# Two accumulators in turn for the inner sums, and a borrowed one for the scores

## The chip, the cores and the metric

One core of a Trainium2 chip runs the whole program. Its engines are named as the profile names them: PE multiplies matrices (PEld is its loading of weights), DVE, ACT and POOL work on vectors, and SP issues most transfers. The metric is device time in microseconds. Three runs of the kernel before took 1115.9, 1118.8 and 1119.08 us, with a median of 1118.8 us.

## The reference

The reference is block-causal attention, and then a feed-forward layer with a gate on all its outputs:

```
scores = q @ k^T / 8                      # 8 batches x 8 heads, 576 x 64 each, float32
scores = where(block_i >= block_j, scores, -1e9)      # blocks of 64 positions
attn   = exp(scores - rowmax); attn = attn / (rowsum + 1e-9)
x      = (attn @ v), heads side by side   # 4608 tokens x 512
h      = x @ w_in                         # 512 x 2048
g      = h * sigmoid(1.702 h)
out    = g @ w_out                        # 2048 x 512
```

## The kernel before

**Attention** goes by pairs of heads; a pair is called a turn here, as in the code, and there are 32, numbered from 0. The scores of a turn stand in five row chunks of growing width (64, 192, 320, 448 and 576 columns). `score` makes them in groups: PE writes the scores of both heads to PSUM banks, `weigh` reduces them on DVE (mask, scale, row minimum; in the profile L351) and takes the exponential on ACT (L358), and `normalise` multiplies by the reciprocal of the row sum, on POOL or DVE. From the ninth turn on `turn` transposes the result on DVE (L385, L390) into `turned`, and after the widest chunk SP issues 16 transfers (L397) that put it into the order in which `av` reads it. `av` multiplies by the values one turn later, and ACT copies the outcome to `xr`.

**The feed-forward layer** goes by 12 tiles of 384 tokens, and by 16 pieces of the 2048 inner columns in each. For each piece PE makes an *inner sum* `hp` (12 matmuls of 384 columns, one PSUM bank), which ACT (tanh, L562) and DVE (L563) turn into `g`; ACT rounds it to `gh` (L571), POOL makes the rest `gl` (L82), and PE adds three products for each of three 128-token blocks to the *outer sums* `acc0` to `acc2` (9 matmuls of 512 columns). Operands are split into a high and a low part, hence three products for each.

**Order.** PE's order is fixed by the code: `keep_in_program_order` holds every matmul where it was written. Inner and outer sums come from a generator that is advanced between the steps of a turn (`advance`). From the tenth turn on a turn is `"3+0/2+1 - - - V - - 4 - - - L -"`: one score group of chunks 3 and 0 and of 2 and 1, then the values of the turn before (`V`), then the widest chunk 4 as a group, then the next turn's q and k (`L`). The generator stops only where an inner sum has just been made, so a score group stands between an inner sum and the outer sum of the piece before. Six inner sums fall into each turn. They are called *first* to *sixth* here, counted from the score group 3+0/2+1: first, second, `V`, third, fourth, score group 4, fifth, sixth. The order on DVE, ACT and POOL is made by a scheduler from priorities and dependencies; `tc.high_priority` favours the gate (tanh, `g`, `gh`, `gl`).

**PSUM** has eight banks. Three hold `acc0` to `acc2`, one (`h`) holds every inner sum in turn, and four (`w0` to `w3`) go round for scores and values from the tenth turn on. `w3` serves the conversion of the weights before that. A tile that takes a bank waits until all that read the bank's last tile are done.

Of the kernel before, what the change touches and what calls it, by code (L numbers as in the profile page):

```python
# [10 lines left out]
F32 = mybir.dt.float32  # L11
# [29 lines left out]
def attention_moe_kernel(  # L41
# [12 lines left out]
    P = 128  # L54
# [9 lines left out]
    HP = H // 2  # L64
# [4 lines left out]
    ps = ctx.enter_context(tc.tile_pool(name="ps", bufs=1, space=PSUM))  # L69
# [4 lines left out]
    def early(n):  # L74

        return n < 2 * HP
# [7 lines left out]


    turns = {"n": 0, "bank": 0, "experts": False}
    conv = {"step": 0, "loaded": 0}

    def bank():
        tags = ["w0", "w1", "w2"]  # L90
        if not turns["experts"]:
            tags += ["acc0", "acc1", "acc2", "h"]
        elif turns["n"] > 2 * HP:
            tags.append("w3")
        turns["bank"] += 1
        return ps.tile([P, 512], F32, tag=tags[turns["bank"] % len(tags)], name="bank")

    def mm(**kw):
        return tc.keep_in_program_order(nc.tensor.matmul(**kw))  # L99
# [65 lines left out]
    def width(i):  # L165
        return BLK * (2 * i + 1)

    def qrange(i):
        return (0, BLK) if i == 0 else (BLK * (2 * i - 1), BLK * (2 * i + 1))
# [135 lines left out]
    def score(n, banks):  # L305

        if n not in stats:
            mx = d2.tile([P, NCH + 1, 2], F32, tag="mx", name="mx")
            sm = d2.tile([P, NCH, 2], F32, tag="sm", name="sm")
            stats[n] = (mx, sm)  # L310
        todo = []
        for chunks in banks:

            part = []
            for lo, hi in ((0, 512),) if width(chunks[0]) <= 512 else ((0, 256), (256, S)):
                ss = [bank() for _ in range(2)]
                c = 0
                for i in chunks:
                    a, z = qrange(i)
                    w = min(hi, width(i)) - lo  # L320
                    for hd in range(2):
                        r = slice(hd * D, hd * D + D)

                        mm(
                            out=ss[hd][:, c : c + w], lhsT=qk[n][r, 0, a : a + P],
                            rhs=qk[n][r, 1, lo : lo + w], start=True, stop=True,
                        )
                        part.append((i, hd, lo, lo + w, ss[hd][0 : z - a, c : c + w]))
                    c += w
            todo.append(sorted(part, key=lambda x: (chunks[::-1].index(x[0]), x[2])))  # L330
        for chunks, part in zip(banks, todo):
            e = {}
            for i, hd, lo, hi, s in part:
                e[i] = weigh(n, i, hd, lo, hi, s, e.get(i))
            for i in chunks[::-1]:
                normalise(n, i, e[i])
                if not early(n):
                    turn(n, i, e[i])

    def weigh(n, i, hd, lo, hi, s, e):  # L340
        mx, sm = stats[n]
        a, z = qrange(i)
        m = z - a
        w = width(i)
        if early(n):
            e = es[i]
        elif e is None:
            e = d2.tile([P, 2, w], F32, tag=f"e{i % 2}", name="e", bufs=1)
        last = i > 0 and hi == w
        mk = mask[0:m, MW - (hi - lo) : MW] if last else mask[0:m, 0 : hi - lo]  # L350
        nc.vector.tensor_tensor_reduce(  # L351
            out=e[0:m, hd, lo:hi], in0=s, in1=mk,
            op0=ALU.add, op1=ALU.min, scale=-0.125,
            scalar=3e38 if lo == 0 else mx[0:m, NCH, hd : hd + 1],
            accum_out=mx[0:m, i, hd : hd + 1] if hi == w else mx[0:m, NCH, hd : hd + 1],
        )
        if hi == w:
            nc.scalar.activation(  # L358
                out=e[0:m, hd], in_=e[0:m, hd], func=AF.Exp, scale=-1.0,
                bias=mx[0:m, i, hd : hd + 1], accum_out=sm[0:m, i, hd : hd + 1],  # L360
            )
        return e

    def normalise(n, i, e):
        _, sm = stats[n]
        m = BLK if i == 0 else P
        c = sm[0:m, i]
        nc.vector.tensor_scalar(
            out=c, in0=c, scalar1=1e-9, scalar2=2.0, op0=ALU.add, op1=ALU.mult
        )  # L370
        nc.vector.reciprocal(out=c, in_=c)  # L371
        on = SCALE_ON[phase(n)][i]
        for hd in range(2):
            x, sc = e[0:m, hd], c[:, hd : hd + 1]
            if on == "P":
                nc.gpsimd.tensor_tensor(out=x, in0=x, in1=sc.to_broadcast([m, width(i)]), op=ALU.mult)  # L376
            elif on == "D":
                nc.vector.tensor_scalar(out=x, in0=x, scalar1=sc, scalar2=None, op0=ALU.mult)  # L378
            else:
                nc.scalar.activation(out=x, in_=x, func=AF.Copy, scale=sc)  # L380
# [128 lines left out]
    def moe():  # L509
        prev = None  # L510

        def second(state):
            g_hi, g_lo, fc, acc, t = state
            todo = [(c, ga, wb) for c in range(TILES[t][1] // P) for ga, wb in ((g_hi, "woh"), (g_hi, "wol"), (g_lo, "woh"))]
            if fc < NFC - 1:

                todo.sort(key=lambda x: x[1] is g_lo)
            begun = set()
            for x, (c, ga, wb) in enumerate(todo):
                last = ga is g_lo  # L520
                mm(
                    out=acc[c], lhsT=ga[:, c * P : (c + 1) * P], rhs=weights(wb, fc // FG)[:, fc % FG],
                    start=fc == 0 and c not in begun, stop=fc == NFC - 1 and last,
                )
                begun.add(c)
                if fc == NFC - 1 and last:
                    osb = d2.tile([P, DM], F32, tag="osb", name="osb", bufs=3)
                    nc.scalar.copy(out=osb, in_=acc[c])  # L528
                    r = TILES[t][0] + c * P
                    nc.sync.dma_start(out=out[r : r + P, :], in_=osb)  # L530
                if x % 3 == 2:
                    yield 650

        for t in range(NT):
            tt = TILES[t][1]
            if t == 0:
                yield ("tile", 0)
                split(0)
            xh, xl = xs["xh"], xs["xl"]
            acc = [ps.tile([P, DM], F32, tag=f"acc{c}", name=f"acc{c}") for c in range(tt // P)]  # L540
            for fc in range(NFC):
                if t == 0:
                    convert(fc // FG * GROUP + NDC + fc % FG + 1)
                hp = ps.tile([P, 512], F32, tag="h", name="hp")
                fs = slice(fc % FG * P, (fc % FG + 1) * P)
                terms = [(wa, xb, dc) for dc in range(NDC) for wa, xb in (("wih", xh), ("wil", xh), ("wih", xl))]
                if fc == 0:

                    terms.sort(key=lambda x: x[1] is xl)
                for cnt, (wa, xb, dc) in enumerate(terms):  # L550
                    mm(
                        out=hp[:, 0:tt], lhsT=weights(wa, fc // FG)[:, dc, fs], rhs=xb[:, dc, 0:tt],
                        start=cnt == 0, stop=cnt == 3 * NDC - 1,
                    )
                    if cnt % 3 == 2:
                        yield unit1(tt)
                g = d2.tile([P, TT], F32, tag="g", name="g", bufs=1)[:, 0:tt]
                gh = d2.tile([P, TT], F32R, tag="gh", name="gh")[:, 0:tt]
                gl = d2.tile([P, TT], F32R, tag="gl", name="gl")[:, 0:tt]

                with tc.high_priority(offset=300):
                    nc.scalar.activation(out=g, in_=hp[:, 0:tt], func=AF.Tanh, scale=1.702)  # L562
                    nc.vector.scalar_tensor_tensor(  # L563
                        out=g, in0=g, scalar=1.0, in1=hp[:, 0:tt], op0=ALU.add, op1=ALU.mult
                    )

                if fc == NFC - 1 and t + 1 < NT:
                    yield ("tile", t + 1)
                    split(t + 1)
                with tc.high_priority(offset=300):  # L570
                    nc.scalar.copy(out=gh, in_=g)  # L571
                    subtract(nc.gpsimd, gl, g, f(gh))
                yield ("gate", fc)
                if prev is not None:
                    yield from second(prev)
                prev = (gh, gl, fc, acc, t)
        yield from second(prev)
# [87 lines left out]
```

## Time and profile before

| What | Value |
|---|---|
| median of three runs | 1118.8 us (1115.9 to 1119.08) |
| profiled execution | 1116.9 us, its span; it lies between the runs |
| instructions | 19972 |
| PE busy | 1082.2 us, 97% |
| PE loading weights | 912.9 us, 82% |
| DVE, ACT, POOL busy | 584.2, 498.9 and 406.4 us (52%, 45%, 36%) |
| PE on the chain that ended last | 30% of the span |

The profile is of one execution on the core. A row of the groups or of the timeline gives the line of the code, the engine, the operation, the tiles (output, arrow, inputs), the shape and the count; the last column names who ended the idle time before it. A wait is put down to the engine whose signal came last. Matmuls overlap, and their ends are modelled, so that a busy PE can still stand late by a fraction of a microsecond; the chain of waits shows that in the length of a stretch of twelve or nine matmuls.

### The profile page before, as it was taken

How to read it: one execution, taken by the hardware profiler on the slowest of the kernel's cores; microseconds unless marked ns; L12 is line 12 of the kernel's file. 1: busy time of each engine (PE TensorE's matmuls, PEld its weight loads, DVE VectorE, ACT ScalarE, POOL GpSimd, SP SyncE). 2: the span in 40 equal slices, each digit the busy share in tenths (PEclk: the TensorE clock that was granted, in tenths of full speed). 3: DMA queues.
4: the chain of work that ended last, by engine and by line, in shares of the span. 5: the costliest groups of instructions: out<-in, count | busy, mean ns of one | idle time of the engine just before them, and what ended most of it. 6: DMA issues, size and time to landing. Idle time of an engine off the chain costs nothing. (4 is left out here: it accounts for less than half of the span.)

```text
span 1116.9 us, 19972 instructions
## 1 busy us (share of the span) xinstructions
PE 1082.2 (97%) x6960; PEld 912.9 (82%) x6960; DVE 584.2 (52%) x1856; ACT 498.9 (45%) x1321; POOL 406.4 (36%) x509
## 2 busy tenths in 40 slices
PE   6979999999999999999999999999999999999998
PEld 4757777788888888888888888888888888899997
DVE  6786786655645645655555555645645654211210
ACT  5865775443533534534443443443444434322322
POOL 4665565332333333333333332333333333122222
PEclk8979999999999999999999999999999999999999
DMA  8634523342434433243443333344442332200000
GB/s 183 193 89 153 146 61 80 72 103 59 96 81 86 109 80 70 58 99 71 113 86 75 80 92 68 63 108 86 86 103 66 71 84 54 54 30 1 29 1 29
DMA packets 219365, 91.25 MB, mean 82 GB/s; under 512 B 197760, under 2 KB 197760, under 8 KB 219264
## 3 DMA queue, kind: packets, MB, share of 16 engines
q1 hardware_dynamic: 214528, 89.38, 34.1%
q8 instruction: 55, 0.90, 0.3%
q10 hardware_dynamic: 4736, 0.59, 0.3%
q14 instruction: 46, 0.38, 0.1%
HBM read 45.09 MB, written 9.44 MB: 49 GB/s over the span
## 5 line engine op out<-in xcount | busy, mean ns | idle before, releaser
L82 POOL TENSOR_TENSOR gl<-g,gh 128x384 fp32r<-128x384 f32 x192 | 194.5, 1013 | 555.1 <-ACT gh L571 450.4
L563 DVE SCALAR_TENSOR_TENSOR g<-g,hp 128x384 f32<-128x384 f32 x192 | 106.0, 552 | 318.6 <-ACT g L562 317.2
L99 PE MATMUL hp<-xh,wih 128*128 128x384 f32 x768 | 265.8, 346 | 2.8 <-DVE g L563 1.8
L562 ACT ACTIVATE g<-hp 128x384 f32<-128x384 f32 x192 | 94.2, 491 | 368.5 <-PE hp L99 361.0
L99 PE MATMUL hp<-xh,wil 128*128 128x384 f32 x768 | 258.7, 337 | 0.0
L99 PE MATMUL hp<-xl,wih 128*128 128x384 f32 x768 | 254.4, 338 | 0.2
L99 PE MATMUL acc<-woh,gh 128*128 128x512 f32 x576 | 233.9, 406 | 0.0
L99 PE MATMUL acc<-wol,gh 128*128 128x512 f32 x576 | 227.0, 394 | 0.0
L99 PEld LDWEIGHTS hp<-xh,wih 128*128 128x128 f32 x768 | 144.4, 188 | 30.9 <-DVE g L563 20.3
L99 PE MATMUL acc<-woh,gl 128*128 128x512 f32 x576 | 168.2, 393 | 0.3 <-POOL gl L82 0.3
L571 ACT CAST gh<-g 128x384 fp32r<-128x384 f32 x192 | 98.4, 513 | 156.8 <-DVE g L563 156.5
L99 PEld LDWEIGHTS hp<-xh,wil 128*128 128x128 f32 x768 | 144.6, 188 | 5.6
L358 ACT ACTIVATE e<-e,mx 64x64 f32<-64x64 f32 (+4 forms) x240 | 132.2, 552 | 32.2 <-DVE mx L351 32.2
L376 POOL TENSOR_TENSOR e<-e,sm 64x64 f32<-64x64 f32 (+1 forms) x192 | 113.6, 612 | 86.3 <-DVE sm L371 42.5
L99 PEld LDWEIGHTS hp<-xl,wih 128*128 128x128 f32 x768 | 144.0, 188 | 1.0 <-DVE xl L82 1.0
L99 PE MATMUL bank<-qk 64*128 64x320 f32 (+4 forms) x768 | 124.3, 432 | 16.2 <-DVE qk L297 10.4
L99 PEld LDWEIGHTS acc<-woh,gh 128*128 128x128 f32 x576 | 108.2, 188 | 34.2 <-issue 10.8
L99 PEld LDWEIGHTS acc<-woh,gl 128*128 128x128 f32 x576 | 107.6, 188 | 25.4 <-POOL gl L82 1.2
L351 DVE CUSTOM_DVE_ANT_0 e<-bank,mask 64x64 f32<-64x64 f32 (+4 forms) x240 | 89.7, 417 | 70.1 <-PE bank L99 67.0
L99 PEld LDWEIGHTS acc<-wol,gh 128*128 128x128 f32 x576 | 108.4, 188 | 16.8 <-issue 0.4
L385 DVE STREAM_TRANSPOSE turned<-e 128x384 f32<-128x384 f32 (+1 forms) x192 | 92.5, 500 | 49.5 <-POOL e L376 48.9
L99 PEld LDWEIGHTS bank<-qk 64*128 64x128 f32 x768 | 71.4, 196 | 56.4 <-issue 25.4
(50 smaller groups left out, 960.6 us busy)
## 6 DMA issues: line engine op xcount, KB each, us to landing
turned<-turned SPq DMA_DIRECT2D x192, 80.0 KB, 2.1
turned<-turned SPq DMA_DIRECT2D x96, 112.0 KB, 2.2
raw<-in_q_dram SPq DMA_DIRECT2D x128, 72.0 KB, 2.3
out_dram<-osb SPq DMA_DIRECT2D x36, 256.0 KB, 2.4
raw<-in_k_dram SPq DMA_DIRECT2D x120, 72.0 KB, 2.4
turned<-turned SPq DMA_DIRECT2D x96, 88.0 KB, 2.1
words<-in_moe_w_in_dram SPq DMA_DIRECT2D x16, 512.0 KB, 5.6
vp<-in_v_dram SPq DMA_DIRECT2D x60, 128.0 KB, 2.4
```

The source lines that it names most:

```text
L82: eng.tensor_tensor(out=out, in0=in0, in1=in1, op=ALU.subtract)
L99: return tc.keep_in_program_order(nc.tensor.matmul(**kw))
L351: nc.vector.tensor_tensor_reduce(out=e[0:m, hd, lo:hi], in0=s, in1=mk, op0=ALU.add, op1=ALU.min, scale=-0.125, scalar=3e38 if lo == 0 else ...
L358: nc.scalar.activation(out=e[0:m, hd], in_=e[0:m, hd], func=AF.Exp, scale=-1.0, bias=mx[0:m, i, hd : hd + 1], accum_out=sm[0:m, i, hd : hd ...
L376: nc.gpsimd.tensor_tensor(out=x, in0=x, in1=sc.to_broadcast([m, width(i)]), op=ALU.mult)
L385: nc.vector.transpose(out=tw[:, :, SLOT[i] : SLOT[i] + i, hd].rearrange("p b j c -> p j b c"), in_=e[:, hd, 0 : i * P],)
L562: nc.scalar.activation(out=g, in_=hp[:, 0:tt], func=AF.Tanh, scale=1.702)
L563: nc.vector.scalar_tensor_tensor(out=g, in0=g, scalar=1.0, in1=hp[:, 0:tt], op0=ALU.add, op1=ALU.mult)
L571: nc.scalar.copy(out=gh, in_=g)
```

## The change

From the tenth turn on an inner sum no longer always goes to bank `h`. `h` and `w3` are kept as a pair, one "now" and one "spare", and each inner sum takes the other one than the inner sum before. The rotation for scores and values goes over three banks, `w0` to `w2`, instead of four. A score step takes four banks, and the fourth is now lent from the pair: it is the spare one. After such a loan the next inner sum stays on the bank that the last one used; the one after that takes the bank that was lent.

```diff
     turns = {"n": 0, "bank": 0, "experts": False}
+    gate_bank = {"now": "h", "spare": "w3", "lent": False}
     conv = {"step": 0, "loaded": 0}
 
     def bank():
         tags = ["w0", "w1", "w2"]
         if not turns["experts"]:
             tags += ["acc0", "acc1", "acc2", "h"]
-        elif turns["n"] > 2 * HP:
-            tags.append("w3")
         turns["bank"] += 1
         return ps.tile([P, 512], F32, tag=tags[turns["bank"] % len(tags)], name="bank")
+
+    def lent_bank():
+        gate_bank["lent"] = True
+        return ps.tile([P, 512], F32, tag=gate_bank["spare"], name="bank")
+
+    def next_hp():
+        if turns["n"] > 2 * HP and not gate_bank["lent"]:
+            gate_bank["now"], gate_bank["spare"] = gate_bank["spare"], gate_bank["now"]
+        gate_bank["lent"] = False
+        return ps.tile([P, 512], F32, tag=gate_bank["now"], name="hp")
...
         todo = []
+        taken = 0
         for chunks in banks:
 
             part = []
             for lo, hi in ((0, 512),) if width(chunks[0]) <= 512 else ((0, 256), (256, S)):
-                ss = [bank() for _ in range(2)]
+                ss = []
+                for _ in range(2):
+                    taken += 1
+                    ss.append(lent_bank() if taken == 4 and turns["n"] > 2 * HP else bank())
                 c = 0
...
-                hp = ps.tile([P, 512], F32, tag="h", name="hp")
+                hp = next_hp()
```

PE's matmuls stand in the same order as before. DVE, ACT and POOL keep their instructions too, but the scheduler sets one gate of each turn, that of the second inner sum, behind the softmax of chunks 1 and 2.

On DVE, between the score group 3+0/2+1 and its second half, before (L563 makes `g`, L385 and L390 transpose, L351 reduces scores):

```order
L371 RECIPROCAL sm<-sm 128x2
L390 STREAM_TRANSPOSE turned<-e 64x2x2x32
L563 SCALAR_TENSOR_TENSOR g<-g,hp 128x384
L390 STREAM_TRANSPOSE turned<-e 64x2x2x32
L563 SCALAR_TENSOR_TENSOR g<-g,hp 128x384
L385 STREAM_TRANSPOSE turned<-e 128x3x4x32 x2
L351 ISA e,mx<-bank,mask 128x192
L351 ISA mx 128x1
L351 ISA e,mx<-bank,mask 128x192
L351 ISA mx 128x1
L351 ISA e,mx<-bank,mask 128x320
```

And there in the changed kernel (L576 makes `g`, L398 and L403 transpose, L364 reduces scores):

```order
L384 RECIPROCAL sm<-sm 128x2
L403 STREAM_TRANSPOSE turned<-e 64x2x2x32
L576 SCALAR_TENSOR_TENSOR g<-g,hp 128x384
L403 STREAM_TRANSPOSE turned<-e 64x2x2x32
L398 STREAM_TRANSPOSE turned<-e 128x3x4x32 x2
L364 ISA e,mx<-bank,mask 128x192
L364 ISA mx 128x1
L364 ISA e,mx<-bank,mask 128x192
L364 ISA mx 128x1
L364 ISA e,mx<-bank,mask 128x320
```

The second `g` row, that of the second inner sum, has gone from ahead of the transposes of chunk 3 to a place behind the transposes of chunk 2, where it stands with the third one; the first `g` row, the transposes and the reductions keep their order among themselves.

On ACT at the same place, before (L562 tanh, L571 `gh`, L358 exponentials, L451 and L450 copies of the values' product):

```order
L358 ACTIVATE e,sm<-e,mx 128x448 x2
L562 ACTIVATE g<-hp 128x384
L571 CAST gh<-g 128x384
L562 ACTIVATE g<-hp 128x384
L571 CAST gh<-g 128x384
L358 ACTIVATE e,sm<-e,mx 128x192 x2
L358 ACTIVATE e,sm<-e,mx 128x320 x2
L451 COPY xr<-bank 128x512
```

And in the changed kernel (L575 tanh, L584 `gh`, L371 exponentials, L464 copies):

```order
L371 ACTIVATE e,sm<-e,mx 128x448 x2
L575 ACTIVATE g<-hp 128x384
L584 CAST gh<-g 128x384
L371 ACTIVATE e,sm<-e,mx 128x192 x2
L371 ACTIVATE e,sm<-e,mx 128x320 x2
L575 ACTIVATE g<-hp 128x384
L584 CAST gh<-g 128x384
L464 COPY xr<-bank 128x512
```

The second tanh and the second `gh` have changed places with the exponentials of chunks 1 and 2.

## The prediction

> **What bounds the kernel now.** I read the engines' shares first, then the stretches from the tenth turn's score group to the last one's end (213 to 954 us) and from there on.
>
> ```profile
> PE 1082.2 (97%) x6960; PEld 912.9 (82%) x6960; DVE 584.2 (52%) x1856; ACT 498.9 (45%) x1321; POOL 406.4 (36%) x509
> ```
>
> ```profile
> 213.00:954.00 741.00, 740.74 (x4832) 627.74 (x4832) 404.88 (x1341) 310.57 (x838) 248.55 (x322) 1.00 0.37 83
> 954.00:1117.00 163.00, 158.37 (x835) 142.35 (x833) 24.66 (x45) 46.48 (x93) 37.59 (x37) 1.00 0.07 22
> ```
>
> In the 741 us that the change touches PE is busy for 740.74, while DVE, the next, is busy for 404.88. So PE's own queue sets the time there, and whatever PE waits is added to it. Small waits hide in a busy row. The chain that ended last shows them, since it gives each stretch of PE its length; here is one turn of it (start, length).
>
> ```profile
> 822.89 2.37 PE hp L99 x12
> 825.26 2.04 PE bank L99 x16
> 827.30 2.24 PE acc L99 x9
> 829.54 2.10 PE hp L99 x12
> 831.65 2.08 PE acc L99 x9
> 833.73 2.11 PE hp L99 x12
> 835.84 2.92 PE bank L99 x60
> 838.75 2.26 PE acc L99 x9
> 841.02 2.10 PE hp L99 x12
> 843.12 2.09 PE acc L99 x9
> 845.21 2.24 PE hp L99 x12
> 847.45 1.17 PE bank L99 x8
> ...
> 855.08 2.36 PE hp L99 x12
> 857.44 2.04 PE bank L99 x16
> ```
>
> The turn lasts 857.44 - 825.26 = 32.18 us. An undisturbed inner sum takes 2.10. The one ahead of the score group 3+0/2+1 (the sixth of the turn before, at 822.89) takes 2.37, the fourth (845.21) 2.24: they wait for their bank. PE's weight loads name the cause:
>
> ```profile
> PEld hp L99 <- DVE g L563: 20.3, 48, 2.0
> ```
>
> That is 48 first weight loads held until DVE had made `g` from the only bank, about two in each of 23 turns. The 20.3 us are the loads' wait, most of it behind matmuls that still ran; what PE loses is 0.27 + 0.14 = 0.41 us in the turn shown.
>
> **What the change removes.** With two banks the fourth and sixth inner sums no longer wait for the `g` just ahead. That takes away 0.41 us a turn, 23 x 0.41 = 9.4 us in all, if nothing comes in its place. The matmuls themselves are the same.
>
> **What it adds.** Follow the pair of banks through a turn. The score group lends the spare bank to its fourth tile, which is head 1 of chunks 2 and 1. The first inner sum stays on its bank. The second takes the lent bank, so it now waits for the last reduction of chunk 2. In the kernel before nobody was in a hurry for that reduction:
>
> ```profile
> 832.27 0.56 DVE L563 SCALAR_TENSOR_TENSOR g<-g,hp 128x384 f32<-128x384 f32 x1 [2.56 <-ACT g L562]
> 832.86 0.31 DVE L390 STREAM_TRANSPOSE turned<-e 64x128 f32<-64x128 f32 x1
> 836.46 0.55 DVE L563 SCALAR_TENSOR_TENSOR g<-g,hp 128x384 f32<-128x384 f32 x1 [3.29 <-ACT g L562]
> 836.93 1.03 DVE L385 STREAM_TRANSPOSE turned<-e 128x384 f32<-128x384 f32 x2
> ...
> 839.07 0.49 DVE L351 CUSTOM_DVE_ANT_0 e<-bank,mask 128x320 f32<-128x320 f32 x1
> ...
> 844.14 0.31 DVE L390 STREAM_TRANSPOSE turned<-e 64x128 f32<-64x128 f32 x1
> ```
>
> The reduction ended at 839.07 + 0.49 = 839.56; the second inner sum started at 833.73. It ran 14 us after its scores because chunk 1 goes into the buffer that chunk 3 leaves (`e1`, one buffer), so the two transposes of chunk 3 come first. The new order on DVE takes the second `g` (836.46) out from ahead of them. They can then follow the short transpose, 832.86 + 0.31 = 833.17, but they also wait for all sixteen transfers that read `turned` for the turn before:
>
> ```profile
> 821.94 10.07 SPq L397 DMA_DIRECT2D turned<-turned  x16
> ```
>
> ```profile
> 918.52 11.80 SPq L397 DMA_DIRECT2D turned<-turned  x16
> ```
>
> ```profile
> DMA to landing us min/median/max: 2.0/2.1/4.1
> ```
>
> Sixteen issues in 10.07 us are 0.63 apart; the last starts at 821.94 + 15 x 0.63 = 831.4 and lands 2.1 later, at 833.5. From there the transposes and reductions need what they took before, 839.56 - 836.93 = 2.63 us: the bank is free at about 836.2 and PE stands from 833.73 until then, **2.5 us**. Without the transfers it would be 833.17 + 2.63 = 835.8, 2.1 us; that is the lower end. In some turns other transfers come between the sixteen, up to 11.80 us (the last turn), which is 1.7 more; I take 0.5 as the mean. And since the sixth inner sum now starts 0.27 sooner while the transfers start when they did, PE is there 0.27 earlier and waits that much longer. Idle per turn: 2.5 + 0.5 + 0.27 = 3.3 us. The matmul after a late start is itself late, as with the old waits; 0.1. Behind the waiting matmul PE holds everything: the second sum, the values, the outer sums, and with score group 4 also the next turn's transfers, so nothing catches up.
>
> Net of the waits removed: 3.3 + 0.1 - 0.41 = 3.0 us a turn, 23 x 3.0 = **69 us**.
>
> **What costs nothing.** The second `g` moves behind the transpose at 844.14. With the reductions done 3.4 us sooner (836.2 for 839.56) that transpose ends at 841.0; `g`, `gh` and `gl` follow. Its outer sums are due after a sum from 836.2, the values, an outer sum and the third sum (2.11 + 2.92 + 2.26 + 2.10): 845.6. That is 4.6 us of cover. If it were gone, the outer sums would wait for `gh`. Score group 4 lends a bank too. Its last reductions follow the group at 847.45, and the sixth sum, which takes that bank, comes at 855.08; the row below has it free at 850.29, 4.8 us ahead. Three banks for scores and values are enough for the same reason: the values at 835.84 take banks of chunks 3 and 0, whose reductions stand on DVE ahead of the idle 2.56 us before 832.27, so end by 829.7. On SP only two loads of values change places.
>
> ```profile
> 849.74 0.55 DVE L351 CUSTOM_DVE_ANT_0 e<-bank,mask,mx 128x320 f32<-128x320 f32 x1
> ```
>
> **The clock.** Such stands slow PE afterwards. The trace's granted clock changes on a grid of 3.41 us, so I cut the early part, where PE stood for DVE and ACT, on that grid (length, PE's busy time; the clock is the third number from the end):
>
> ```profile
> 26.22:29.63 3.41, 1.83 (x24) 1.32 (x26) 3.41 (x10) 2.39 (x6) 2.74 (x5) 1.00 0.83 328
> 29.63:33.04 3.41, 3.41 (x44) 3.41 (x38) 2.00 (x8) 1.63 (x4) 2.99 (x4) 0.50 0.02 7
> ...
> 80.83:84.24 3.41, 1.59 (x6) 1.09 (x7) 2.34 (x5) 2.05 (x4) 1.51 (x2) 1.00 0.00 0
> 84.24:87.66 3.42, 3.42 (x12) 3.23 (x11) 1.80 (x4) 0.56 (x2) 0.78 (x1) 0.50 0.00 0
> 87.66:91.07 3.41, 3.41 (x16) 2.10 (x14) 2.18 (x6) 1.40 (x3) 2.24 (x2) 1.00 0.00 0
> ...
> 200.30:203.71 3.41, 2.22 (x11) 1.21 (x9) 2.62 (x7) 0.74 (x2) 1.16 (x2) 1.00 0.12 26
> 203.71:207.13 3.42, 2.01 (x8) 1.44 (x9) 3.34 (x12) 1.67 (x4) 1.00 (x1) 1.00 0.00 0
> 207.13:210.50 3.37, 3.37 (x19) 3.06 (x18) 3.30 (x9) 1.72 (x5) 0.00 (x0) 1.00 0.27 44
> ```
>
> A stretch with 1.58 us or more of idle PE (1.83 of 3.41 busy) is followed by half clock; 1.41 idle (2.01 of 3.42) is not. And a stretch at half clock in which PE is not quite full is followed by another:
>
> ```profile
> 15.98:19.39 3.41, 3.39 (x19) 2.56 (x17) 2.22 (x10) 2.58 (x11) 2.87 (x4) 0.50 0.68 133
> 19.39:22.80 3.41, 3.41 (x14) 2.53 (x15) 2.48 (x9) 3.03 (x9) 2.30 (x3) 0.50 0.82 131
> ```
>
> Inner matmuls start 0.32 us apart at half clock,
>
> ```profile
> 84.56 0.52 PE L99 MATMUL hp<-xl,wih 128*128 128x384 f32 x1
> 84.88 0.52 PE L99 MATMUL hp<-xh,wih 128*128 128x384 f32 x1
> ```
>
> against 2.10 / 12 = 0.175, so a full slow stretch loses 3.41 x (1 - 0.175 / 0.32) = 1.55 us. A stand of 3.1 us (3.3 less the modelled tail of the last matmul) falls anywhere on the grid, and nearly always puts 1.5 us into one stretch. If that is the stretch in which it ends (a little over half the cases), one slow stretch follows: 1.55. Otherwise the stretch in which it ends is slow, not full, and followed by another: about 2.7. The mean is 2.0, and 23 x 2.0 = **46 us**. The bounds are nothing and 23 x 2.7 = 62.
>
> The Trainium skill ("TensorE: Matmul & The Clock Gate", section "Why this matters for your kernels") asks for no idle of PE over some 3 us, and lets one idle window of 3.4 us lower the clock. By that rule stands below a whole window cost no clock, and the sum would be the second rival's; the stretch from 80.83 with 1.59 us busy speaks against it.
>
> **Sum.** 1116.9 (the profiled execution; the runs shown have a median 1.9 above it, within their spread) + 69 + 46 = 1232; I say **1230 us**.
>
> **The rivals.**
> *The clock stays up.* Then 1116.9 + 69 = 1186. For it: the one pause late in the first part, around 203.7, kept the clock although it was over 2 us in all. Against it: there the grid cut it in two parts below 1.5, which 3.1 us don't allow.
> *Faster: the lent bank is free in time.* If chunk 2's reduction ended before 833.73, the old waits would go and nothing come: 1116.9 - 9.4 = 1107. It decides at 833.73 - 2.63 = 831.1, when the transposes of chunk 3 would have to start. For it: DVE is idle for the 2.56 us before 832.27. Against it: the last transfer is only issued at 831.4, and `g` and the short transpose hold DVE until 833.17.
> *No difference.* The stand is absorbed by a slack of PE that I don't see; 740.74 of 741 us busy leaves none. It would give 1117.
> *The clock hardly recovers.* If the values' 60 small matmuls don't count as a full stretch, one or two more slow stretches follow, 1.55 to 3.1 us: 1116.9 + 69 + 46 + 23 x 1.55 = 1268 or more.
>
> **How the numbers follow.** The forecast has 0.70, with its own range of 1205 to 1250; the clock that stays up 0.17, the hardly recovering clock 0.06, faster 0.05, no difference 0.02. The range 1180 to 1248 takes in the second case and nearly all of the first and leaves out under 2 in 10. About 0.3%, 3.4 us, is what a measurement of this kernel can tell from no change; beyond it slower has 0.70 + 0.17 + 0.06 = 0.93.
>
> **What would show it.** Right: PE idle before inner sums for some 3 us, 23 times, released by DVE's reduction of scores (now L364), the waits on `g` nearly gone, a turn of about 37 us, a granted clock below 1.00 behind each stand. A turn of 35 us with the clock at 1.00 would leave the first sum right and the clock wrong; a turn of 31.8 us would make the whole forecast wrong.

## The result, and the profile after

The changed kernel takes 1220.3 us (median of four runs, 1217.9 to 1222.5), the kernel before in the same comparison 1118.9 us. The ratio is 1.092, with a 95% interval of 1.0903 to 1.0937: slower by 9.2%, 101 us. The forecast was 1230 us, with a range of 1180 to 1248.

The profiled execution has a span of 1216.1 us. The page's line of shares:

```profile
PE 1104.4 (91%) x6960; PEld 938.6 (77%) x6960; DVE 587.1 (48%) x1856; ACT 499.5 (41%) x1321; POOL 406.5 (33%) x509
```

PE has the same 6960 matmuls as before, and two things happened to it. It is busy for 22 us more (1104.4 against 1082.2) with the same work, and its share falls from 97% to 91%, so it also stands idle. The waits of PE and of its weight loads say for what (us in total, times, longest):

```profile
PEld hp L108 <- DVE mx L364: 87.9, 23, 5.0
PE hp L108 <- DVE mx L364: 77.8, 23, 4.5
PEld hp L108 <- DVE g L576: 2.3, 2, 2.0
```

Of the 48 waits of weight loads for `g` 2 are left. In their place stand 23, one in each turn, for the reduction of scores (L364): 77.8 us of idle PE, 3.38 us each.

The windows from the tenth turn's score group to the end of the last, and from there on:

```profile
213.00:1052.00 839.00, 761.17 (x4823) 651.62 (x4823) 407.83 (x1341) 311.22 (x838) 247.64 (x321) 0.96 0.33 73
1052.00:1217.00 165.00, 159.99 (x844) 144.00 (x842) 24.68 (x45) 46.51 (x94) 38.60 (x38) 1.00 0.08 24
```

The 741 us have become 839, and the rest is as it was (165 against 163). Per turn it is 839 / 23 = 36.5 us for 32.2. The mean granted clock there is 0.96.

One stand on the timeline (start, length, engine, line, operation, tiles; in brackets the idle time ahead and what ended it):

```profile
440.07 0.59 SPq L410 DMA_DIRECT2D turned<-turned  x1
...
440.66 0.56 DVE L576 SCALAR_TENSOR_TENSOR g<-g,hp 128x384 f32<-128x384 f32 x1 [2.56 <-ACT g L575]
...
441.25 0.31 DVE L403 STREAM_TRANSPOSE turned<-e 64x128 f32<-64x128 f32 x1
441.27 0.86 PE L108 MATMUL acc<-woh,gl 128*128 128x512 f32 x3
...
442.36 1.04 DVE L398 STREAM_TRANSPOSE turned<-e 128x384 f32<-128x384 f32 x2 [0.80 <-issue]
443.54 0.36 DVE L364 CUSTOM_DVE_ANT_0 e<-bank,mask 128x192 f32<-128x192 f32 x1
...
444.92 0.08 DVE L364 DVE_READ_ACCUMULATOR2_ANT mx<- 128x1 f32 x1
...
445.06 0.44 PE L108 MATMUL hp<-xh,wih 128*128 128x384 f32 x1 [2.93 <-DVE mx L364]
```

It is the row of causes that the prediction drew. The outer sum ends at 442.13, and the second inner sum could start. SP has issued the last of the sixteen transfers at 440.07; DVE's short transpose ends at 441.56, and DVE then idles for 0.80 us. The transfers land 2.1 us after their issue (the median), the last one so at about 442.2. The profile names no releaser for this idle stretch, but in 19 of the 23 turns it names the transfers (23.5 us in all; the row stands below, with the run that moves four of them). Only now, at 442.36, come the two transposes of chunk 3, which free `e1`, and then the reductions of chunks 1 and 2. The last one is read out at 445.00, and PE starts at 445.06.

The chain of that turn (start, length) shows the second cost:

```profile
445.06 3.41 PE hp L108 x12
448.46 3.40 PE bank L108 x60
451.86 2.25 PE acc L108 x9
454.11 2.10 PE hp L108 x12
```

The inner sum behind the stand takes 3.41 us where an undisturbed one takes 2.10, and the values 3.40 for 2.92. The clock explains it. Here is the clock's grid (length, busy PE; the clock is the third number from the end) around two stands:

```profile
333.39:336.80 3.41, 0.81 (x5) 0.81 (x6) 2.74 (x12) 1.87 (x7) 0.68 (x2) 1.00 0.68 109
336.80:340.21 3.41, 3.41 (x19) 2.97 (x20) 1.85 (x7) 0.69 (x3) 2.03 (x4) 0.50 0.03 7
340.21:343.63 3.42, 3.42 (x60) 3.22 (x57) 1.17 (x3) 1.21 (x3) 1.00 (x1) 1.00 0.00 0
...
879.52:882.93 3.41, 1.62 (x7) 0.96 (x6) 1.83 (x4) 0.63 (x2) 0.99 (x1) 1.00 0.60 115
882.93:886.35 3.42, 1.69 (x10) 1.69 (x11) 2.40 (x13) 2.75 (x10) 0.97 (x2) 1.00 0.43 69
886.35:889.76 3.41, 3.41 (x64) 3.16 (x62) 2.49 (x8) 1.43 (x4) 1.58 (x2) 1.00 0.02 5
```

In the first, 2.60 us of idle fall into one stretch, and the next one runs at half clock. In the second the grid cuts a stand into 3.41 - 1.62 = 1.79 and 3.42 - 1.69 = 1.73, and the clock stays up. Counted so over the 23 stands, 16 lowered the clock, two of them for two stretches: 18 slow stretches. At 1.55 us each that is 28 us.

### The profile page after: what moved, and what is told of

Same layout as the page of the kernel before. It is cut to its first block, busy times and chain, and to the rows that moved or that the text cites. A ratio compares the mean times of both kernels' runs of the same rounds, so it can differ in the third digit from the quotient of the medians.

```text
span 1216.1 us, 19995 instructions
## 1 busy us (share of the span) xinstructions
PE 1104.4 (91%) x6960; PEld 938.6 (77%) x6960; DVE 587.1 (48%) x1856; ACT 499.5 (41%) x1321; POOL 406.5 (33%) x509
## 4 chain that ended last, share of the span: by engine, by line
PE 42%; SPq 17%; DVE 15%; issue 5%; DMA 3%; ACT 1%; DVEq 0%; POOL 0%; POOLq 0%; ACTq 0%
PE hp L108 20%; SPq L410 17%; PE acc L108 14%; PE bank L108 8%; DVE e L364 4%; DVE turned L398 4%; DMA turned<-turned 3%; DVE qk L306 2%; DVE e L391 2%; DVE turned L403 1%; DMA raw<-in_q_dram 0%; ACT e L371 0%; DVE g L576 0%; DVE mx L364 0%; DVE sm L384 0%
## 5 line engine op out<-in xcount | busy, mean ns | idle before, releaser
L108 PE MATMUL hp<-xh,wih 128*128 128x384 f32 x768 | 271.5, 353 | 80.3 <-DVE mx L364 77.8
L576 DVE SCALAR_TENSOR_TENSOR g<-g,hp 128x384 f32<-128x384 f32 x192 | 106.0, 552 | 378.6 <-ACT g L575 377.3
L108 PE MATMUL hp<-xh,wil 128*128 128x384 f32 x768 | 267.0, 348 | 0.0
L108 PE MATMUL hp<-xl,wih 128*128 128x384 f32 x768 | 263.1, 350 | 0.2
L575 ACT ACTIVATE g<-hp 128x384 f32<-128x384 f32 x192 | 94.2, 491 | 406.9 <-PE hp L108 401.5
L108 PEld LDWEIGHTS hp<-xh,wih 128*128 128x128 f32 x768 | 149.8, 195 | 101.8 <-DVE mx L364 87.9
L584 ACT CAST gh<-g 128x384 fp32r<-128x384 f32 x192 | 98.5, 513 | 167.7 <-DVE g L576 167.6
L371 ACT ACTIVATE e<-e,mx 64x64 f32<-64x64 f32 (+4 forms) x240 | 132.1, 552 | 69.3 <-DVE mx L364 69.3
L108 PEld LDWEIGHTS hp<-xh,wil 128*128 128x128 f32 x768 | 150.3, 196 | 6.7
L108 PEld LDWEIGHTS hp<-xl,wih 128*128 128x128 f32 x768 | 150.3, 196 | 1.0 <-DVE xl L82 1.0
L398 DVE STREAM_TRANSPOSE turned<-e 128x384 f32<-128x384 f32 (+1 forms) x192 | 92.6, 500 | 76.9 <-POOL e L389 47.4
L364 DVE CUSTOM_DVE_ANT_0 e<-bank,mask 64x64 f32<-64x64 f32 (+4 forms) x240 | 89.7, 417 | 82.8 <-PE bank L108 79.4
```

The costliest lines, as they stand in the source:

```text
L364: nc.vector.tensor_tensor_reduce(out=e[0:m, hd, lo:hi], in0=s, in1=mk, op0=ALU.add, op1=ALU.min, scale=-0.125, scalar=3e38 if lo == 0 else ...
L371: nc.scalar.activation(out=e[0:m, hd], in_=e[0:m, hd], func=AF.Exp, scale=-1.0, bias=mx[0:m, i, hd : hd + 1], accum_out=sm[0:m, i, hd : hd ...
L398: nc.vector.transpose(out=tw[:, :, SLOT[i] : SLOT[i] + i, hd].rearrange("p b j c -> p j b c"), in_=e[:, hd, 0 : i * P],)
L576: nc.vector.scalar_tensor_tensor(out=g, in0=g, scalar=1.0, in1=hp[:, 0:tt], op0=ALU.add, op1=ALU.mult)
```

## The experiments

All of them are edits of the changed kernel, except the one that says otherwise. Ratios are to the kernel before.

### Another tile gets the lent bank

The score group's first tile (head 0 of chunks 3 and 0), whose reductions come first, takes the lent bank instead of the fourth.

```diff
-                    ss.append(lent_bank() if taken == 4 and turns["n"] > 2 * HP else bank())
+                    ss.append(lent_bank() if taken == 1 and turns["n"] > 2 * HP else bank())
```

> The changed kernel, but the score step borrows its first tile (head 0 of chunks 3 and 0) from the pair and not its fourth. Theory (the stand before the second inner sum is the late reduction of the lent tile): head 0 of chunk 3 is reduced about 3 us after the scores start, long before the second inner sum, so the 23 waits of 3.4 us on a reduction of scores vanish and with them the slow stretches of the clock; all old waits of 0.41 us a turn stay away (1117 - 9 = 1108). A smaller wait may come instead: the second bank of the values' product is now one that holds chunks 2 and 1, whose reduction ended at 420.3 where those last matmuls were due at 419.7 in the turn from 406 us; 0.6 us x 23 = 14. So 1108 to 1124 us. Rival (two banks in turn, or only three banks going round, cost the time whatever is lent): it stays above 1180.

Measured: 1128.0 us (1126.6 to 1128.5), ratio 1.008 (1.0063 to 1.0098). PE's wait for reductions in the stretch from 210 to 960 us, and its place on the timeline:

```profile
PE bank L108 <- DVE mx L364: 13.7, 23, 0.7
```

```profile
419.64 2.87 PE L108 MATMUL bank<-turned,vp 128*64 128x128 f32 x56
423.09 0.34 PE L108 MATMUL bank<-turned,vp 128*64 128x64 f32 x4 [0.58 <-DVE mx L364]
```

The inner sums no longer wait, and 92 of the 101 us are gone, so the loan of that one bank is the cause. The order on DVE goes back with it: in this turn the second inner sum's `g` (420.33) stands ahead of chunk 3's transposes (420.80) again, as in the kernel before. The loan to the fourth tile forbids that order, since the second inner sum then needs the reductions behind those transposes. The late reduction is still there. It now sits in a bank of the three that go round, and the values' last four matmuls are the next to want it. That makes 23 short waits of 0.6 us (13.7 / 23), for which the kernel before has none in these turns. The next run, which is without them, takes 19.3 us less (1108.8), 0.84 us a turn, so each stop costs 0.24 us more than the idle that the profile shows. The modelled ends of matmuls may hide that part; no run separates it. This second wait is what lifted the time above the range expected.

### And the values take the spare bank

The same, and the values' second tile is the spare inner bank too.

```diff
-        o, o0 = bank(), bank()
+        o, o0 = bank(), lent_bank() if turns["n"] > 2 * HP else bank()
```

> As the run that lends the first tile, and the second bank of the values' product is borrowed from the pair too, so that nothing needs a bank of chunks 2 and 1 until score group 4. Theory: no stand is left and the old waits are gone: 1117 - 9 = 1108 us (1105 to 1112). Rival (the old waits of 0.41 us a turn were covered, or come back elsewhere): 1117 to 1120, as before.

Measured: 1108.8 us (1107.8 to 1111.3), ratio 0.9914 (0.9894 to 0.9934). The window of the 23 turns:

```profile
213.00:945.00 732.00, 731.50 (x4830) 632.17 (x4829) 406.31 (x1342) 311.67 (x839) 248.85 (x322) 1.00 0.38 84
```

No wait is left in the turns and the clock is at 1.00. 741 - 732 = 9 us, or 0.4 us a turn, is what two banks for the inner sums are worth; the prediction gave them 9.4.

### Three banks, and no turns

The inner sums stay on one bank, as before; scores and values go over three banks, and the fourth tile of a group takes `w3`.

```diff
-        if turns["n"] > 2 * HP and not gate_bank["lent"]:
-            gate_bank["now"], gate_bank["spare"] = gate_bank["spare"], gate_bank["now"]
```

> The changed kernel without the turns: every inner sum goes to one bank as before, the other one of the pair serves the fourth tile of each score step alone, and scores and values go round over three. Theory: that part costs nothing and gains nothing, 1119 us (1116 to 1122), with about 46 waits of inner sums on g as before. Rival (fewer banks for scores and values hold PE up): over 1130, with new waits of matmuls of scores or values.

Measured: 1119.5 us (1116.4 to 1120.0), ratio 1.0002 (0.9991 to 1.0013).

```profile
PEld hp L106 <- DVE g L574: 20.4, 48, 2.0
```

All 48 old waits are back, 20.4 us as before, and there is no new one. The rotation over three costs nothing, as predicted, and the whole loss hangs on an inner sum that takes a bank a score tile has used.

### The stand filled with matmuls that nobody reads

Ahead of the second inner sum 15 more matmuls of 384 columns are made, into the bank that the first one has left. PE does 345 matmuls more.

```diff
+                was = gate_bank["now"]
                 hp = next_hp()
+                if gate_bank["fill"] and gate_bank["now"] != was:
+                    gate_bank["fill"] = False
+                    junk = ps.tile([P, 512], F32, tag=was, name="junk")
+                    for _ in range(15):
+                        mm(out=junk[:, 0:tt], lhsT=..., rhs=xh[:, 0, 0:tt], start=True, stop=True)
```

> The changed kernel, and 15 more matmuls of 384 columns (2.6 us) on PE ahead of each second inner sum, into the bank that nobody uses then; their sums are read by nobody. They fall into the stand, which lasts 3.2 us or more, so they don't lengthen it. Theory (17 slow stretches of the clock cost 17 x 1.55 = 26 us): the waits shrink to under 1.5 us, the clock stays at 1.00 after 230 us, and the time falls to 1220 - 26 = 1194 us (1188 to 1200), although PE does more. Rival (the slow clock costs little, for what it holds back would wait anyway): 1215 to 1225.

Measured: 1194.4 us (1190.8 to 1195.3), ratio 1.0665 (1.0639 to 1.0691).

```profile
PE hp L109 <- DVE mx L365: 19.3, 23, 2.1
```

```profile
213.00:1028.00 815.00, 795.72 (x5168) 689.00 (x5167) 407.04 (x1339) 309.81 (x838) 249.50 (x322) 1.00 0.34 76
```

The time that PE waits for the bank, filled or idle, is what it was: 19.3 us idle and 345 x 0.175 = 60.4 us of matmuls make 79.7, against 77.8. Yet with more work the kernel is 1220.3 - 1194.4 = 26 us faster, and its clock is 1.00. These 26 us are what the lowered clock costs the changed kernel.

### Fewer of them

Six such matmuls instead of 15, in a single run.

> As the filled stand, but with 6 more matmuls of 384 columns (1.05 us) and not 15. The stands shrink from 3.4 to 2.3 us of idle on the mean. Theory (a stretch of 3.41 us is followed by half clock where PE is idle for more than some 1.9 us of it; in the changed kernel 1.80 was not and 1.93 was): fewer of the 23 stands lower the clock, some 4 to 12 slow stretches instead of 17, and 1197 to 1213 us. Rival (any stand of over 1.5 us does, as the early part of the program made me think): 15 or more slow stretches, 1215 or more.

Measured: 1218.1 us. The theory missed, and the rival's numbers came: 16 slow stretches. The rival's rule, that any stand of over 1.5 us lowers the clock, did not hold either: all 23 stands have 1.77 us of idle or more, and seven of them kept it.

```profile
PE hp L109 <- DVE mx L365: 53.7, 23, 3.6
```

```profile
259.80:263.22 3.42, 1.65 (x10) 1.32 (x9) 2.54 (x13) 2.08 (x8) 0.90 (x3) 1.00 0.66 108
263.22:266.63 3.41, 3.41 (x22) 2.97 (x22) 2.05 (x7) 0.49 (x1) 1.78 (x3) 0.50 0.02 5
```

53.7 us idle and 138 x 0.175 = 24.2 us of matmuls are again 77.8: the bank comes free when it did. The stands are shorter, 2.3 us on average, but half of them now lie whole in one stretch. There 1.77 us of idle (3.42 - 1.65) were enough to lower the clock. How long a stand is does not decide, then; how much of it falls into one stretch does.

### Four of the sixteen transfers from ACT's queue

The four transfers of the last quarter are issued by ACT, so that SP is done sooner.

```diff
-                    nc.sync.dma_start(
+                    (nc.scalar if kb == 3 and turns["n"] > 2 * HP else nc.sync).dma_start(
```

> The changed kernel, but from the tenth turn on 4 of the 16 transfers that rearrange a turn's result are issued by ACT and not by SP, side by side with SP's first ones. SP's last issue then starts 4 x 0.63 = 2.5 us sooner. Theory (in 19 of 23 turns the transfers set when chunk 3 is transposed): the transposes start when the short transpose is through, 8.0 us after the score group, and not at 8.7 to 10.4; the stands fall from 3.4 to about 2.2 us of idle, 23 x 1.2 = 28 us less, and with fewer slow stretches of the clock (from 17 to some 6, 17 us less) 1175 to 1195 us. Rival (the reductions, not the transfers, set the size): under 10 us less, 1210 or more.

Measured: 1179.4 us (1176.1 to 1180.6), ratio 1.0548 (1.0522 to 1.0575).

```profile
DVE turned L398 <- DMA turned<-turned: 2.0, 1, 2.0
PE hp L108 <- DVE mx L364: 51.4, 23, 4.1
```

In the changed kernel the first of these two rows reads:

```profile
DVE turned L398 <- DMA turned<-turned: 23.5, 19, 2.4
```

So the transfers are off the path, and what is left is what the prediction gave as the lower end: transposes behind the short transpose, then reductions. Nearly all stands are 2.15 us long, near the 2.1 of that lower end:

```profile
397.51 0.45 PE L108 MATMUL hp<-xh,wih 128*128 128x384 f32 x1 [2.15 <-DVE mx L364]
```

The 41 us come from both terms: 77.8 - 51.4 = 26.4 us of stand, and 9 slow stretches instead of 18, 9 x 1.55 = 14 us. Because the stands are so alike here, they show where the clock's border lies:

```profile
361.47:364.88 3.41, 1.55 (x9) 1.55 (x10) 2.38 (x13) 2.08 (x8) 1.45 (x3) 1.00 0.23 38
364.88:368.29 3.41, 3.41 (x61) 3.16 (x61) 2.15 (x8) 0.49 (x1) 1.40 (x2) 1.00 0.02 5
395.60:399.02 3.42, 1.51 (x9) 1.51 (x10) 2.39 (x13) 2.46 (x9) 1.52 (x3) 1.00 0.98 276
399.02:402.43 3.41, 3.41 (x29) 2.97 (x30) 2.15 (x8) 0.49 (x1) 1.40 (x2) 0.50 0.07 26
```

With 3.41 - 1.55 = 1.86 us of idle the clock stays; with 3.42 - 1.51 = 1.91 it falls.

### A buffer of its own for chunk 1

If the reductions of chunks 1 and 2 are late because chunk 1 waits for `e1`, another buffer for it must take the stand away. Chunk 1 gets the buffer `wm`, which only the conversion of the weights used.

```diff
-            e = d2.tile([P, 2, w], F32, tag=f"e{i % 2}", name="e", bufs=1)
+            e = d2.tile([P, 2, w], F32, tag="wm" if i == 1 else f"e{i % 2}", name="e", bufs=1)
```

> The changed kernel with its fourth tile lent as it is, but chunk 1 gets a buffer of its own (that of the converted weights, done with by then) in place of the one that chunk 3 leaves. Theory (the lent bank is late because chunk 1 waits for chunk 3's transposes, and they for the transfers): the reductions of chunks 1 and 2 no longer wait for either; the last stands on DVE right behind the first inner sum's g, which ended at 413.94 in the turn from 406.3 us, so it ends near 414.4 where the second inner sum is due at 414.7. The stands are gone or under 0.3 us, the clock stays at 1.00, 1108 to 1116 us. Rival (the loan itself holds PE, whatever the buffer): above 1180.

Measured: 1104.6 us (1103.3 to 1106.5), ratio 0.9884 (0.9866 to 0.9901). It beats both kernels. The reductions on DVE:

```profile
405.38 0.49 DVE L364 CUSTOM_DVE_ANT_0 e<-bank,mask 128x320 f32<-128x320 f32 x1
...
406.61 0.56 DVE L576 SCALAR_TENSOR_TENSOR g<-g,hp 128x384 f32<-128x384 f32 x1 [0.74 <-ACT g L575]
```

and the window from 213 us to the end of the turns:

```profile
213.00:940.00 727.00, 727.00 (x4808) 628.65 (x4807) 396.85 (x1324) 305.60 (x826) 244.90 (x319) 1.00 0.37 84
```

The last reduction now stands ahead of the first `g` instead of behind the transposes, the lent bank is free in time, and PE never stops: 727.00 of 727.00 us. The buffer was the cause of the lateness. The time came out below what was expected, and a second place was a reason. The ninth turn also waits for a late reduction, in the kernel before and here:

```profile
205.12 0.80 PE L99 MATMUL bank<-qk 64*128 64x320 f32 x2 [2.60 <-DVE mx L351]
```

```profile
200.51 0.80 PE L108 MATMUL bank<-qk 64*128 64x320 f32 x2 [0.17 <-DVE mx L364]
```

2.43 us of that wait are gone, and the tenth turn's score group starts at 208.43 us instead of 213.02. The other 2.2 us of this difference are not the buffer's. The score group ahead of that wait already starts at 185.87 us instead of 188.05, and it does so at 185.89 in the run with four transfers on ACT's queue, which has the old buffers. Those two profiled executions have 6 slow stretches of the clock ahead of it, the kernel before has 8. The wait can cost a slow stretch too: in seven of the nine executions profiled with the old buffers there one follows it, and from that score group to the tenth turn's it is then about 26.5 us, for 24.97 in the profile of the kernel before and 22.56 here. So ahead of the tenth turn the buffer is worth 2.4 us, and about 4 where the clock falls.

### What of it is the buffer, and what the second bank

Two runs take the last version apart: the kernel before with the buffer, and the changed kernel with the buffer from the tenth turn on only (`"wm" if i == 1 and turns["n"] > 2 * HP`).

> The kernel before (one bank for the inner sums) with a buffer of its own for chunk 1, so that its reductions no longer wait for chunk 3. Theory: the 14 us that the two banks with this buffer gain consist of 4.6 us ahead of the tenth turn (its first score group came at 208.4 us instead of 213.0), which the buffer alone brings, and 22 x 0.44 = 9.7 us from the old waits on g, which only the second bank takes away: here 1119 - 4.6 = 1114 us (1111 to 1117), a turn of 32.2 us, and still 48 waits of the weight loads on g. Rival: the buffer itself does all of it: 1105 to 1108.

> The changed kernel with a buffer of its own for chunk 1 only from the tenth turn on. Theory: the early part stays as it was (first score group of the tenth turn at about 213 us), the turns last 31.8 us with no wait for the lent bank: 1119 - 9.7 = 1109 us (1107 to 1112). Rival: the gain of the early part is made by the second bank or by a shift of phase, and stays: 1104 to 1106.

Measured: the buffer alone 1111.7 us (1110.4 to 1112.8), ratio 0.9944 (0.9924 to 0.9963); the banks with the buffer from the tenth turn 1109.7 us (1109.1 to 1110.6), ratio 0.9923 (0.9904 to 0.9942). The second is as the theory had it. The first is inside the theory's range of 1111 to 1117, but its waits are not as expected:

```profile
PEld hp L99 <- DVE g L563: 13.9, 29, 2.0
```

With its reductions done early DVE makes one of the two late `g` of a turn in time in most turns even with a single bank: 29 waits for 48, and a turn of 32.05 us for 32.22 (means of 22 turns). That part the theory had given to the second bank alone, and the 4.6 us that it gave to the buffer ahead of the tenth turn were in part the clock's. Against the kernel before in the same comparison (1118.0 us) the two runs gain 6.3 and 8.4 us; the banks with the buffer from the start gained 12.6 in theirs (1104.6 against 1117.2).

## Why the prediction was right, and where its size was off

**Sign, place and mechanism were right.** One bank is lent, its last reader is late because chunk 1 waits for a buffer, and PE stands ahead of the second inner sum, 23 times. The loan to another tile, three banks without turns, the buffer and the transfers each took away the part that the prediction's chain of causes gave them.

**The waits removed** were worth 0.41 us a turn, 9.4 us in all, as predicted: the second experiment has them alone and gains 9 us in its window.

**What costs nothing** cost nothing: the rotation over three banks alone ran at a ratio of 1.0002 (it costs something only where the late tile goes round in it, as in the first experiment), and neither the second `g` nor score group 4's loan shows as a wait of PE.

**The stand** was a little under-sized: 3.1 us of idle were predicted, 77.8 / 23 = 3.38 measured. From the last issue to PE's start I had put 2.1 + 2.63 = 4.73 us; in the turn shown it is 445.06 - 440.07 = 4.99, since DVE does not start its transposes at the landing. The other transfers were allowed 0.5, and the mean is 3.38 - 2.93 = 0.45 above this turn. The 0.2 for the modelled tail and the 0.1 for the late matmul were estimates; the first two experiments together give 0.24 for both at the stop that they show. With 3.38 + 0.2 + 0.1 - 0.41 = 3.27 the net term is 3.27 x 23 = 75 us, predicted 69.

**The clock was the term that failed**, by its size: 23 x 2.0 = 46 us predicted, 26 measured by filling the stand, 28 by counting slow stretches. Two steps of it were wrong. *"Nearly always puts 1.5 us into one stretch"* took the border from the early part, where 1.58 us of idle had lowered the clock. Here 1.86 did not, so that a stand that the grid cuts into two like parts costs no clock: seven of the 23. And *"otherwise the stretch in which it ends is slow, not full, and followed by another"* was to happen in nearly half of the stands. Five ended in a slow stretch, and only the two that left much idle in it were followed by another. A view of the grid of the changed kernel with one of each kind:

```profile
626.93:630.35 3.42, 2.93 (x9) 2.93 (x10) 2.04 (x11) 1.51 (x6) 1.25 (x3) 0.50 0.17 26
630.35:633.76 3.41, 3.41 (x62) 3.16 (x63) 1.75 (x4) 1.00 (x2) 1.40 (x3) 1.00 0.00 0
...
736.16:739.57 3.41, 1.71 (x5) 1.71 (x6) 2.38 (x13) 2.07 (x8) 0.97 (x2) 0.50 0.50 83
739.57:742.99 3.42, 3.42 (x20) 2.98 (x21) 2.17 (x8) 0.49 (x1) 1.40 (x2) 0.50 0.00 0
```

With 0.49 us of idle in the slow stretch the clock came back; with 1.70 it did not. The forecast was 1232 by its sum; 20 less for the clock and 6 more for the stands make 1218, beside 1216 for the profiled execution and 1220 for the median.

**The rivals.** A clock that stays up (the first in the prediction's list, and the one it means by "the second rival") would have given 1186; the stands cost 26 us through the clock alone, and the run that keeps it up by filling them takes 1194. The Trainium skill ("TensorE: Matmul & The Clock Gate", section "Why this matters for your kernels") warns of idle over some 3 us; here 1.77 us within one stretch of 3.41 lowered it. The Trainium skill ("TensorE: Matmul & The Clock Gate", section "A second HAM failure mode: psum-queue depth-cycling") tells of a kernel that goes through PSUM banks and in which short idles between groups of matmuls make the clock go up and down. That short idles do it is nearer to what these rows show; the change of banks alone does not do it here, since with two banks in turn and no stand PE is busy for 727.00 of 727.00 us at a clock of 1.00. The rival of a bank that is free in time was wrong here, and its time, 1107, is about what the versions take in which the bank is free: 1108.8 and 1109.7. A change that makes no difference and a clock that hardly recovers are excluded, the last by the full clock in the stretch behind the values (340.21).

## What to carry to other kernels

Before a buffer is lent, follow its borrower's last reader back to what holds that reader: here a reduction that nobody was in a hurry for hung, through a single buffer, on sixteen transfers of the turn before. In the turns, freeing the reader (one more buffer) and choosing other borrowers were worth the same, 1109.7 and 1108.8 us; the buffer gained more (1104.6) where it also took away a wait ahead of them. The same edit, two banks in turn, went from 9.2% slower to 1.2% faster with it. A stand of PE is to be costed with its clock, which added a third here (26 us to 78).

## What the runs showed of the hardware that was not expected

PE's clock went by how much of one 3.41-us stretch PE stood, and not by how long the stand was. The border lay between 1.86 us (kept) and 1.91 (lowered) where the stand began in the stretch before, and 1.77 lowered it where the whole stand lay in one stretch. The modelled ends of matmuls, which hide some 0.2 us at each stop, may be the reason for that difference; it was not tried. In the early part 1.58 us had been enough, and a slow stretch with 3.39 us of 3.41 busy had been followed by another, where 2.93 of 3.42 sufficed above. Small matmuls for the attention stand in those stretches; why they differ is open.

Matmuls that nobody reads, put into a stand, made the kernel 26 us faster; six in place of 15 left it within its spread (one run), with 16 slow stretches for 18.

The clock of the first 190 us differs from execution to execution, though the edits, the new buffer apart, begin only with the tenth turn: the profiles have 5 to 8 slow stretches there, and the score group ahead of the ninth turn's last wait starts anywhere from 185.0 to 188.05 us. A difference of some 3 us between two single profiles can come from that alone.
